# A chunked linear-attention recurrence and an expert mixture on one core: the triangular solves are placed one unit further ahead of their merge, x of four units is placed by products, TensorE gets filler products

## The chip, the core and the metric

The kernel runs on one NeuronCore of a Trainium2 chip. That core has TensorE (PE in the profile: matrix products into PSUM; PEld is its weight load), VectorE (DVE), ScalarE (ACT), GpSimd (POOL) and SyncE (SP), which here only issues DMAs. The metric is device time in microseconds: the median of the runs shown.

## The reference

All arrays are float32: batch B = 4, H = 8 heads, S = 768 tokens, head size D = 40. The first block is a recurrence over the tokens, for every batch and head:

```python
for t in range(S):
    y[:, :, t] = einsum('bhd,bhde->bhe', r_t, state)
    Sa = einsum('bhde,bhe->bhd', state, a_t)
    state = state * w_t[:, :, None, :] - einsum('bhd,bhe->bhde', Sa, b_t)
    state = state + einsum('bhd,bhe->bhde', v_t, k_t)
```

The second block takes x = y as a 3072 x 320 matrix (one row for each batch and token) and mixes four experts, with the probabilities of a row scaled to a sum of one:

```python
for e in range(4):
    h = maximum(x @ w1[e], 0)          # 320 x 1024
    out += p[:, e:e+1] * (h @ w2[e])   # 1024 x 320
```

## The kernel before

**Units.** The tokens are cut into 12 chunks of 64. A unit is one chunk of two batches, so that 2 x 64 tokens fill the 128 partitions; there are 24 units, two to a chunk (units 0 and 1 are chunk 0, and so on). `q.start` marks chunk 0, in which the state is still zero.

**The attention of a unit** is written as three generators, whose `yield`s are the places at which the code that calls them may stop.

- `within(q)` (L337) needs nothing of other units. It turns w (tile pw), scans it into running products G, turns G back (pg), scales a, b and k with it (gp and its reciprocal on VectorE, then tiles a_tok, n_tok, k_tok), turns these and r and v on TensorE (L368), and forms the 64 x 64 products F, E (pfe) and the scores (pc). F is the strictly triangular matrix whose inverse is needed. Its end forms EV (pev).
- `substitute(q, eng)` (L437) is the **solve**: the 32 x 32 blocks on the diagonal of F are gathered (blocks, L441), transposed in one instruction of VectorE (M, L445) and inverted by forward substitution, 16 steps of a product (L470) and a sum. On VectorE the sum is one reduction (L480), on GpSimd two additions (L483).
- `merge(q)` (L490) makes the 64 x 64 inverse QT of the two blocks: two transposes on VectorE (Qc, QTc), four copies on GpSimd (L503), then products pY and pQ on TensorE with a ScalarE copy behind each.
- `step(q)` (L530) is the part that hangs on the state, in five stages: prn and RH; psat (with SaT and SX behind it); pxr; pdy with Y and the new state; and stage five, which puts Y, that lies by head, into xT, that lies by the 320 columns. For unit 0 stage five is products with 0/1 matrices `pick` (pxT, L624) and one copy; for all others it is 10 to 12 DMAs on SP's queue (L636).

**The mixture** is cut into pieces that wait in the list `todo`, and `mix(n)` emits the next n. Units 0 and 1 go one by one (`mixture_of_unit`: `ups(e)` L651/L659 makes h, `down(e)` L698 the second product). From chunk 1 on, a whole chunk is mixed at once with a Strassen-like scheme (`mixture_of_chunk`, L763), which needs sums and differences of the blocks of w2 (`add_weights`, L735, five VectorE instructions for each expert) and of h (L757). Pieces of w1 come by DMA (`load_piece`, L237), w2 stays in SBUF (L254).

**What sets the order.** The loop from L879 on takes u = 1 to 23. In one turn it emits the first part of `within` of unit u+2, the rest of `within` of u+1, the last stages of `step` of u, all of `merge` and two stages of `step` of u+1, and the solve of u+2, with four gaps between them; `gap(n)` emits `add_weights` where `weights_at` says so, and then one or two pieces of the mixture (one where `sparse` says so). The first half of a solve is emitted at the end of a turn, the second at the start of the next one (the `yield` at L467), and its merge begins in that turn before gap 1. The solves of units 0, 3, 4 and 5 are on VectorE, the other twenty on GpSimd. The text of the program is a priority, not the order: each engine runs a queue that was fixed when the kernel was built, in which a later instruction may stand before an earlier one that is waiting. Instructions under `tc.keep_in_program_order` keep their order among themselves on their engine.

## Time and profile before

The median of three runs is 1178.29 us (1177.43 to 1181.34). The profiled execution took 1181.41 us, and its span on the core is 1179.7 us.

| | PE | PEld | DVE | ACT | POOL |
|---|---|---|---|---|---|
| busy us over the span | 1129.8 | 1005.5 | 698.1 | 364.5 | 462.4 |
| busy us, 5 to 50 us | 25.57 | 21.87 | 29.95 | 11.81 | 10.45 |
| busy us, 225 to 1030 us | 803.69 | 727.43 | 491.62 | 267.20 | 387.61 |

The mean granted clock of TensorE is 0.973; it is 0.70 from 5 to 50 us and 1.00 from 225 to 1030 us.

How to read it: in the table of stretches each line has the stretch and its length in us, then for each engine the busy us and, in brackets, the number of instructions, then the granted clock of TensorE (1.00 is full speed), the busy share of the 16 DMA engines, and GB/s. In the timeline a row has the start and the length in us, engine, line, operation, written tile <- read tiles, shapes and number of merged instructions, and in square brackets how long the engine had been idle before and what released it. A float32 product on TensorE shows as two MATMUL records, a transpose as one.

### The profile page before, as it was taken

The page shows a single profiled execution, that of the slowest core. Times are in us where ns is not written, and L with a number is a line of the kernel's source. Part 1 is how long each engine was busy: PE and PEld are TensorE (multiplying, and loading weights), DVE is VectorE, ACT ScalarE, POOL GpSimd, SP SyncE. Part 2 cuts the span into 40 slices and gives each one's busy share as a digit, 9 for nine tenths or more (in the row PEclk, how much of TensorE's full clock was granted, in tenths as well). Part 3 has the DMA queues.
Part 4 walks back from the last instruction along what each step waited for, and adds up shares of the span by engine and source line. Part 5 has one row for each costly group of instructions (what it writes and reads, how often), then busy time and mean ns, then how long its engine had stood idle before and what let it go on. Part 6 is the DMA issues. An engine that isn't in the chain of part 4 may idle for free.

```text
span 1179.7 us, 38554 instructions
## 1 busy us (share of the span) xinstructions
PE 1129.8 (96%) x16272; PEld 1005.5 (85%) x16272; DVE 698.1 (59%) x1503; ACT 364.5 (31%) x910; POOL 462.4 (39%) x1200
## 2 busy tenths in 40 slices
PE   4789996999999999999999999999999999999998
PEld 3668785899989989898998989999888998988887
DVE  6633787856646655755656566566466557543333
ACT  2323342333332333333333333333323333221110
POOL 4165000044734734625536436447347356250000
PEclk8689997999999999999999999999999999999999
DMA  4782633333333333342342332333333331221330
GB/s 67 200 239 68 141 64 86 78 108 68 95 94 84 96 95 81 92 103 73 95 95 63 108 89 73 107 78 89 90 93 90 93 91 58 76 86 51 103 89 12
DMA packets 220246, 108.03 MB, mean 92 GB/s; under 512 B 164090, under 2 KB 193450, under 8 KB 220074
## 3 DMA queue, kind: packets, MB, share of 16 engines
q1 hardware_dynamic: 220074, 105.56, 34.9%
q8 instruction: 129, 2.11, 0.7%
q14 instruction: 43, 0.35, 0.1%
HBM read 97.04 MB, written 3.93 MB: 86 GB/s over the span
## 4 chain that ended last, share of the span: by engine, by line
PE 86%; DVE 5%; POOL 3%; SPq 2%; issue 2%; DMA 1%; ACT 1%; POOLq 0%; DVEq 0%; ACTq 0%
PE p L763 27%; PE ph L659 27%; PE ph L651 8%; PE pdy L326 3%; PE po L698 2%; PE pfe L326 2%; PE prn L326 2%; POOL Z L483 2%; PE psat L326 2%; PE pxr L326 2%; SPq L188 1%; PE pQ L522 1%; PE pY L510 1%; POOL Z L470 1%; PE pc L326 1%
## 5 line engine op out<-in xcount | busy, mean ns | idle before, releaser
L659 PE MATMUL ph<-xT,w1p 128*128 128x256 f32 (+1 forms) x1520 | 342.8, 378 | 0.2 <-issue 0.2
L659 PEld LDWEIGHTS ph<-xT,w1p 128*128 128x128 f32 x1520 | 274.1, 190 | 62.8 <-issue 25.5
L757 DVE TENSOR_TENSOR a<-hs 128x512 f32<-128x512 f32 x220 | 149.9, 698 | 196.4 <-ACT hs L664 196.3
L483 POOL TENSOR_TENSOR Z<-Z 128x54 f32<-128x54 f32 (+14 forms) x640 | 217.4, 340 | 50.2
L664 ACT ACTIVATE hs<-ph 128x512 f32<-128x512 f32 (+1 forms) x208 | 117.4, 564 | 324.6 <-PE ph L659 323.5
L470 POOL TENSOR_TENSOR Z<-M,Z 128x62 f32<-128x62 f32 (+7 forms) x320 | 154.2, 482 | 89.5 <-DVE M L461 66.0
L677 DVE SCALAR_TENSOR_TENSOR osb<-p,gate,osb 128x320 f32<-128x320 f32 (+1 forms) x242 | 108.4, 486 | 110.4 <-PE p L763 103.2
L763 PE MATMUL p<-sums,a 128*128 128x160 f32 x1056 | 164.8, 299 | 0.0
L763 PEld LDWEIGHTS p<-sums,a 128*128 128x128 f32 x1056 | 152.9, 190 | 2.2
L441 POOL COPY blocks<-F 32x256 f32<-32x256 f32 x80 | 32.3, 404 | 276.6 <-ACT F L416 274.1
L651 PE MATMUL ph<-xT,w1p 64*128 64x256 f32 (+1 forms) x760 | 109.2, 399 | 4.9 <-issue 4.9
L503 POOL COPY QT<-QTc 32x256 f32<-32x256 f32 x96 | 37.7, 393 | 170.6 <-DVE QTc L497 160.7
L763 PE MATMUL p<-w,hs 128*128 128x160 f32 x704 | 102.8, 299 | 0.0
L763 PE MATMUL p<-w,a 128*128 128x160 f32 x704 | 102.8, 299 | 0.0
L763 PEld LDWEIGHTS p<-w,hs 128*128 128x128 f32 x704 | 100.3, 190 | 2.2
L763 PEld LDWEIGHTS p<-w,a 128*128 128x128 f32 x704 | 98.0, 190 | 0.0
L651 PEld LDWEIGHTS ph<-xT,w1p 64*128 64x128 f32 x760 | 67.3, 188 | 17.7 <-issue 7.8
L445 DVE STREAM_TRANSPOSE M<-blocks 128x1024 f32<-128x1024 f32 x24 | 47.1, 1964 | 26.0 <-POOL blocks L441 25.9
L364 DVE RECIPROCAL gp<-gp 128x320 f32<-128x320 f32 x24 | 51.5, 2145 | 0.0
L416 ACT COPY F<-pfe 128x256 f32<-128x256 f32 x48 | 15.5, 375 | 107.8 <-PE pfe L326 107.8
L592 ACT COPY RS<-pxr 64x256 f32<-64x256 f32 x88 | 32.2, 366 | 44.3 <-issue 25.3
L698 PE MATMUL po<-w,hs 128*128 128x320 f32 x128 | 44.0, 500 | 0.0
(140 smaller groups left out, 1406.8 us busy)
## 6 DMA issues: line engine op xcount, KB each, us to landing
w1p<-in_moe_w_dram SPq DMA_DIRECT2D x95, 512.0 KB
w1p<-in_moe_w_dram SPq DMA_DIRECT2D x190, 64.0 KB
w<-in_moe_w_dram SPq DMA_DIRECT2D x4, 1280.0 KB
sums<-in_moe_w_dram SPq DMA_DIRECT2D x9, 512.0 KB
natW<-in_w_dram SPq DMA_DIRECT2D x48, 80.0 KB
natA<-in_a_dram SPq DMA_DIRECT2D x48, 80.0 KB
natB<-in_b_dram SPq DMA_DIRECT2D x48, 80.0 KB
natK<-in_k_dram SPq DMA_DIRECT2D x48, 80.0 KB
```

What stands on the lines that cost most here:

```text
L326: nc.tensor.matmul(out=p[row][half(col), lo + at * out_cols:lo + (at + 1) * out_cols], lhsT=lhsT, rhs=rhs, start=(n == 0), stop=(n == len( ...
L364: nc.vector.reciprocal(out=gp[:], in_=gp[:])
L445: ins = nc.vector.transpose(out=M[:], in_=cols)
L470: ins = eng.tensor_tensor(out=Z[:, 1:3, 0:n, j + 1:Q], in0=M[:, j:j + 2, None, j + 1:Q].to_broadcast([P, 2, n, m]), in1=Z[:, here, 0:n, j: ...
L483: eng.tensor_tensor(out=z[:, 0], in0=z[:, 0], in1=z[:, x], op=ALU.add)
L651: nc.tensor.matmul(out=ph[i][:, f, :], lhsT=w1.last[i * DT:(i + 1) * DT, f, :], rhs=xT[i * DT:(i + 1) * DT, 2, :], start=(f == 0), stop=False,
L659: nc.tensor.matmul(out=ph[i][:, f, :], lhsT=w1.main[:, g, at * P:(at + 1) * P], rhs=xT[:, g, :], start=False, stop=(g == 1 and f == HF // ...
L664: nc.scalar.activation(out=h[:, i * HF // 2:(i + 1) * HF // 2, 0:n], in_=ph[i][:], func=ACTF.Relu,)
L677: nc.vector.scalar_tensor_tensor(out=to, in0=p, scalar=sc, in1=to, op0=ALU.mult, op1=ALU.add)
L698: nc.tensor.matmul(out=po[:], lhsT=hs[e][f // HF][:, f % HF, 0:P], rhs=w2_sb[e][:, f, :], start=(f == 0), stop=(f == NF - 1),)
L757: nc.vector.tensor_tensor(out=t[:], in0=x, in1=y, op=op)
L763: nc.tensor.matmul(out=p[:, n * HD:(n + 1) * HD], lhsT=a[:, f, :], rhs=b[:, f, :], start=(f == 0), stop=(f == HF - 1),)
```

## The change

- **Solve and merge.** `substitute` is no longer cut in two. In a turn of the loop the solve of u+2 now comes after gap 2, behind the first part (Qc, QTc, QT) of the merge of u+1, which has moved from before gap 1 to behind gap 2; the rest of the merge and two stages of `step` of u+1 follow it.
- **Engines.** Units 0 and 1 are solved on VectorE, units 2 to 23 on GpSimd. The four copies into blocks are now two on VectorE and two on ScalarE for every unit.
- **x.** Stage five of `step` places x by products for units 0 to 3 (`placed`), by DMAs for the rest.
- **Step.** Stage four (pdy, state) is emitted after gap 0 ahead of the next part of `within`. For chunk 0 the products pst of stage two get PSUM banks of their own.
- **Chunk 0.** Unit 1 takes the form of `within` that had been used from unit 2 on, with one more stop.
- **Weights.** `add_weights` stops after each instruction; the 20 instructions are dealt over gaps 1 of u = 2 to 2 of u = 5.
- **Filler.** `keep_warm(n)` emits n products of the identity with itself into a PSUM tile that nobody reads: 6 at the start, 4 behind the first part of unit 0's `within`, 36 behind the second part of unit 1's, all pinned.
- **Start.** The probabilities are loaded behind unit 1's a, b, k, v and r. The order of the calls ahead of the loop is written anew.

```diff
@@ -200,12 +200,13 @@
     minus_gate = const.tile([P, NC, B // 2, E], FP32, name="minus_gate")
     total = const.tile([P, NC, B // 2], FP32, name="total")
 
-    for bp in range(B // 2):
-        for i in range(2):
-            nc.sync.dma_start(
-                out=probs[bp * NC:(bp + 1) * NC, i],
-                in_=moe_domain_probs[(2 * bp + i) * S:(2 * bp + i + 1) * S, :].rearrange("(c t) e -> c t e", t=L),
-            )
+    def load_probs():
+        for bp in range(B // 2):
+            for i in range(2):
+                nc.sync.dma_start(
+                    out=probs[bp * NC:(bp + 1) * NC, i],
+                    in_=moe_domain_probs[(2 * bp + i) * S:(2 * bp + i + 1) * S, :].rearrange("(c t) e -> c t e", t=L),
+                )
 
     class Piece:
         pass
@@ -354,7 +355,7 @@
         nc.vector.tensor_tensor(out=q.gl[:], in0=q.gl[:], in1=G[:, :, L - 1:L], op=ALU.mult)
         yield
 
-        pg = by(turn("pg", tok(G))[:], 64)[:, :, 0:D]
+        pg = by(turn("pg", tok(G), q.u == 2)[:], 64)[:, :, 0:D]
         gp = sb.tile([P, H, D], FP32, name="gp")
         ins = nc.vector.tensor_tensor(out=gp[:], in0=pg, in1=n["W"][:, :, 0:D], op=ALU.mult)
         if q.u == 1:
@@ -381,7 +382,9 @@
                 if q.start:
                     tc.keep_in_program_order(ins)
 
-        if not q.start:
+        if q.u == 1:
+            yield
+        if q.u > 0:
             VT = turn_rv()
             yield
 
@@ -391,7 +394,7 @@
         )
         nc.vector.tensor_tensor(out=q.K[:, :, 0:D], in0=n["K"][:], in1=gp[:], op=ALU.mult)
         q.VC = VCs()
-        if not q.start:
+        if q.u > 0:
             nc.scalar.copy(out=q.VC[:, :, 0:D], in_=n["V"][:, :, 0:D])
         yield
 
@@ -400,7 +403,7 @@
         KT = turned("KT", q.K)
         yield
 
-        if not q.start:
+        if q.u > 0:
             causal_scores(VT)
             yield
 
@@ -419,7 +422,7 @@
             causal(of_slot(ET[:], s), pe[s])
         yield
 
-        if q.start:
+        if q.u == 0:
             tc.keep_in_program_order(nc.scalar.copy(out=q.VC[:, :, 0:D], in_=n["V"][:, :, 0:D]))
         q.EV = EVs()
         pev = quadrants(banks("pev"), 0, BY_TOKENS, D, lambda j, s, i: (
@@ -430,7 +433,7 @@
                 nc.scalar.copy(out=of_slot(q.EV[half(p)], i ^ p)[:, :, 0:D], in_=pev[i][half(p)])
         yield
 
-        if q.start:
+        if q.u == 0:
             causal_scores(turn_rv())
         yield
 
@@ -438,8 +441,8 @@
 
         blocks = sb.tile([P, H, Q], FP32, name="blocks")
         for i in range(P // Q):
-            ins = eng.tensor_copy(out=blocks[quarter(i)], in_=q.F[quarter(i), :, quarter(i % 2)])
-            tc.keep_in_program_order(ins)
+            move = nc.scalar.copy if i >= 2 else nc.vector.tensor_copy
+            tc.keep_in_program_order(move(out=blocks[quarter(i)], in_=q.F[quarter(i), :, quarter(i % 2)]))
         M = sb.tile([P, Q, Q], FP32, name="M")
         cols = blocks[:].rearrange("p h c -> p c h")[:, :, None, :].to_broadcast([P, Q, 4, H])
         ins = nc.vector.transpose(out=M[:], in_=cols)
@@ -463,8 +466,6 @@
         for x in (0, 3) if at_once else (0,):
             tc.keep_in_program_order(eng.tensor_copy(out=Z[:, x], in_=unit_cols[:]))
         for j in range(0, Q, 2):
-            if j == Q // 2:
-                yield
             n, m = j // 4 + 1, Q - 1 - j
             here = 3 * (j // 2 % 2) if at_once else 0
             ins = eng.tensor_tensor(
@@ -472,7 +473,7 @@
                 in1=Z[:, here, 0:n, j:j + 2].rearrange("p k x -> p x k")[:, :, :, None].to_broadcast([P, 2, n, m]),
                 op=ALU.mult,
             )
-            if j in (0, Q // 2):
+            if j == 0:
                 tc.keep_in_program_order(ins)
             z = Z[:, :, 0:n, j + 1:Q]
             if at_once:
@@ -485,7 +486,6 @@
 
             odd, even = (Z[:, x].rearrange("p k (r four) -> p k r four", four=4)[:, :, :, 1:3] for x in (3, 0))
             eng.tensor_copy(out=even, in_=odd)
-        yield
 
     def merge(q):
 
@@ -530,6 +530,8 @@
     def step(q, xT):
 
         st = [state[bb] for bb in q.b]
+
+        placed = q.c < 2
         if q.start:
             RH = q.EV
         else:
@@ -558,7 +560,8 @@
         ))
         SX = SXs()
         if not q.end:
-            pst = quadrants(p, NJ * L, BY_TOKENS, D, lambda j, s, i: (
+            at = (banks("pst"), 0) if q.start else (p, NJ * L)
+            pst = quadrants(*at, BY_TOKENS, D, lambda j, s, i: (
                 i ^ s, i, j, q.QT[half(i ^ s), head(j, s), :], RH[half(i ^ s), head(j, s), 0:D],
             ))
         SaT = sb.tile([P, NJ, 2, L], FP32, name="SaT", tag="step", bufs=3)
@@ -618,7 +621,7 @@
                 nc.vector.tensor_tensor(out=x, in0=x, in1=gl[:, :, i, :].to_broadcast([P, NJ, D]), op=ALU.mult)
         yield
 
-        if q.u == 0:
+        if placed:
             px = big("pxT")
             for n, (g, j) in enumerate(PLACES):
                 nc.tensor.matmul(
@@ -626,7 +629,7 @@
                     start=(n == 0 or PLACES[n - 1][0] != g), stop=(n + 1 == len(PLACES) or PLACES[n + 1][0] != g),
                 )
             nc.scalar.copy(out=xT, in_=px[:, 0:3 * P].rearrange("p (g t) -> p g t", g=3))
-        for h in range(H if q.u else 0):
+        for h in range(0 if placed else H):
             lo = h * D
             while lo < (h + 1) * D:
                 g, o = divmod(lo, P)
@@ -733,6 +736,7 @@
             (b[1, 0], b[1, 0], b[0, 0], ALU.subtract),
         ):
             tc.keep_in_program_order(nc.vector.tensor_tensor(out=to, in0=x, in1=y, op=op))
+            yield
 
     def mixture_of_chunk(qs, xT):
 
@@ -826,12 +830,24 @@
         q.xT = chunks_x[q.c][:, :, q.bp * P:(q.bp + 1) * P]
         return step(q, q.xT)
 
+    warm = big("warm")
+
+    def keep_warm(n):
+
+        for _ in range(n):
+            ins = nc.tensor.matmul(out=warm[:, 0:P], lhsT=ident[:], rhs=ident[:], start=True, stop=True)
+            tc.keep_in_program_order(ins)
+
     ws = [within(units[u]) for u in range(3)]
-    run(ws[0], 2)
+    keep_warm(6)
+    run(ws[0], 1)
+    keep_warm(4)
+    run(ws[0], 1)
     load(units[1], "ABKVR")
+    load_probs()
     run(ws[1], 1)
     run(ws[0], 2)
-    run(substitute(units[0], nc.vector))
+    substitute(units[0], nc.vector)
     run(ws[0], 1)
     set_pick()
     m, s = merge(units[0]), begin_step(0)
@@ -843,6 +859,8 @@
         load_piece()
         load_w2(e)
     run(ws[1], 1)
+    keep_warm(36)
+    run(ws[1], 2)
     load(units[2], "ABK")
     load_piece()
     for e in range(2, E):
@@ -851,31 +869,32 @@
     run(s, 4)
     run(ws[1], 1)
     run(s)
-    run(ws[1], 1)
-    run(substitute(units[1], nc.gpsimd))
+    run(ws[1], 2)
     mixture_of_unit(units[0])
+    substitute(units[1], nc.vector)
     normalize()
     run(ws[2], 1)
     run(ws[1])
+    mix(3)
+    m, s = merge(units[1]), begin_step(1)
+    run(m, 1)
     mix(1)
     run(ws[2], 2)
+    run(m)
     mix(1)
     run(ws[2], 2)
-    mix(1)
-    m, s = merge(units[1]), begin_step(1)
-    run(m, 1)
+    run(s, 2)
     run(ws[2], 1)
     load(begin(3), srcs)
-    run(substitute(units[2], nc.gpsimd))
-    run(m)
+    substitute(units[2], nc.gpsimd)
     mix(1)
-    run(s, 2)
-    mix(1)
-    w_next, solve = ws[2], iter(())
-
-    sparse = [4 * u + n for u in range(1, 4) for n in range(4)] + [16]
-
-    weights_at = {4 * 2 + 2: 0, 4 * 3 + 0: 1, 4 * 3 + 2: 2, 4 * 3 + 3: 3}
+    w_next = ws[2]
+
+    sparse = range(4 * 1, 4 * 4 + 2)
+
+    sums_at = {4 * 2 + n: 1 for n in range(1, 11)}
+    sums_at.update({4 * 4 + 3: 2, 4 * 5 + 0: 3, 4 * 5 + 1: 2, 4 * 5 + 2: 3})
+    sum_ops = (None for e in range(E) for _ in add_weights(e))
     for u in range(1, NU):
         q = units[u]
         m = s_next = w = iter(())
@@ -884,18 +903,17 @@
         if u + 2 < NU:
             w = within(units[u + 2])
 
-        def gap(n):
+        def gap(n, pieces=None):
             at = 4 * u + n
-            if at in weights_at:
-                add_weights(weights_at[at])
-            mix(1 if at in sparse else 2)
+            run(sum_ops, sums_at.get(at, 0))
+            mix((1 if at in sparse else 2) if pieces is None else pieces)
 
         run(w, 1)
         run(w_next)
         run(s, 1)
-        run(solve)
         gap(0)
 
+        run(s, 1)
         run(w, 1)
         run(s)
         if u == 1:
@@ -903,24 +921,23 @@
         elif q.bp:
             mixture_of_chunk(units[u - 1:u + 1], chunks_x[q.c])
         run(w, 1)
-        run(m, 1)
         gap(1)
 
         if u + 3 < NU:
             load(begin(u + 3), srcs)
         run(w, 2)
+        gap(2)
+
+        run(m, 1)
+        run(w, 1)
+        if u + 2 < NU:
+            substitute(units[u + 2], nc.gpsimd)
         run(m, 1)
         run(s_next, 1)
         run(m)
-        gap(2)
-
-        run(w, 1)
+        gap(3, 1)
         run(s_next, 1)
-        if u + 2 < NU:
-
-            solve = substitute(units[u + 2], nc.vector if u < 4 else nc.gpsimd)
-            run(solve, 1)
-        gap(3)
+        mix(0 if 4 * u + 3 in sparse else 1)
         s, w_next = s_next, w
     mix(len(todo))
     for piece in last:

```

## The prediction

> **What bounds the kernel now.** I read the slices of the page first (busy tenths of TensorE and its granted clock, 29.5 us each).
>
> ```profile
> PE   4789996999999999999999999999999999999998
> ...
> PEclk8689997999999999999999999999999999999999
> ```
>
> From the eighth slice on TensorE is busy and at full clock to the end; idle and slow-clock time both lie in the first seven, and the seventh has a hole. The table of stretches puts numbers on it:
>
> ```profile
> 50.00:74.00 24.00, 23.63 (x348) 20.03 (x341) 12.88 (x24) 9.58 (x24) 16.19 (x44) 1.00 0.94 277
> 74.00:90.00 16.00, 12.07 (x156) 7.71 (x148) 5.64 (x9) 2.10 (x6) 9.45 (x32) 0.68 0.82 210
> ...
> 114.00:122.00 8.00, 6.80 (x48) 4.53 (x46) 0.56 (x2) 1.37 (x4) 0.00 (x0) 0.79 0.30 101
> 122.00:179.00 57.00, 54.18 (x1024) 45.87 (x1024) 50.49 (x136) 23.39 (x67) 1.58 (x4) 1.00 0.47 95
> 179.00:198.00 19.00, 14.28 (x270) 11.11 (x272) 12.69 (x25) 4.14 (x11) 1.57 (x4) 0.73 0.26 47
> 198.00:211.00 13.00, 8.48 (x88) 6.45 (x78) 8.32 (x22) 3.07 (x10) 0.00 (x0) 0.74 0.55 146
> 211.00:225.00 14.00, 12.39 (x205) 10.46 (x204) 13.27 (x32) 5.92 (x16) 0.00 (x0) 0.88 0.37 109
> ...
> 225.00:1030.00 805.00, 803.69 (x12046) 727.43 (x12042) 491.62 (x1015) 267.20 (x665) 387.61 (x985) 1.00 0.34 88
> ```
>
> From 225 to 1030 us TensorE is busy 803.69 of 805 us at clock 1.00, while VectorE is at 61% and GpSimd at 48%: moving work among those gains nothing there. A gain can only lie before 225 us. The timeline names what ended the long idle times:
>
> ```profile
> 34.70 1.07 PE L510 MATMUL pY<-QTc,F 32*32 32x32 f32 x32 [11.86 <-DVE QTc L497]
> ...
> 78.17 1.06 PE L510 MATMUL pY<-QTc,F 32*32 32x32 f32 x32 [3.93 <-DVE QTc L497]
> ...
> 184.56 1.11 PE L294 MATMUL pNT<-ident,n_tok 128*128 128x128 f32 x4 [4.72 <-DVE n_tok L389]
> ...
> 203.37 3.02 PE L651 MATMUL ph<-xT,w1p 64*128 64x256 f32 x8 [4.52 <-issue]
> ```
>
> The first two are the solves of units 0 and 1, the third VectorE's queue, the fourth (no releaser named) xT: SP issues its 12 DMAs from 189.2 to 199.4 us, and ups begins behind them.
>
> **What slow clock costs.** After each hole the granted clock is about a half:
>
> ```profile
> 78.00:88.50 10.50, 10.33 (x78) 0.51 0.81 194
> 115.50:119.20 3.70, 3.56 (x16) 0.54 0.15 38
> 184.00:194.30 10.30, 9.74 (x174) 0.50 0.26 48
> 200.90:208.00 7.10, 4.63 (x12) 0.52 0.82 225
> 221.40:225.00 3.60, 3.60 (x60) 0.53 0.33 59
> ```
>
> The second product of a piece (po, L698) takes 6.10 us for 12 instructions from 83.12 us, 0.508 each, and 4.57 us for 16 from 131.32 us, 0.286 each: a ratio of 1.78. So a busy microsecond at half clock holds 1/1.78 of full-speed work, and 44% of it is lost: 4.5, 1.6, 4.3, 2.0 and 1.6 us in these five, 14.0 in all. The idle time of the stretches above (length less PE busy) is 0.4, 3.9, 1.2, 2.8, 4.7, 4.5 and 1.6 us. Together some 33 us are lost between 50 and 225 us.
>
> Here a rule is worth weighing. The idle time of 1.20 us before pQ at 115.64 us and that of 1.41 us before pdy at 220.22 us are each followed by a stretch at clock 0.54 or 0.53. The Trainium skill, "TensorE: Matmul & The Clock Gate", section "Why this matters for your kernels", asks only that idle gaps stay under about 3 us; by it these two would cost their 2.6 us alone, by the rows they cost 5.8. The rows decide: what is left of small waits counts double. The same page (Part 1) advises not to model the warm-up, as under 1% of a kernel; by that the filler could be left out. From 5 to 50 us the clock here is 0.70.
>
> **The change, part by part.**
>
> *Start, 5 to 50 us.* After pg of unit 1, TensorE idles 11.86 us (22.84 to 34.70) until unit 0's solve ends, then works at half clock until about 47 us. The 36 fillers are 72 passes; pxT (L624, 12 passes in 1.50 us at full clock, the last 0.275 long) gives 0.111 us a pass, so 8.0 us at full and 14.2 at half clock. If the clock rises after some 3.6 us (the shortest slow stretch above), 18 passes run at half clock and 54 at full, 9.6 us in all, and the fill ends at 32.4, ahead of 34.7. Then the chain from QTc to the first ups (34.56 to 51.66 us) runs at full clock. Its TensorE pieces take 1.07 (pY), 1.44 (pQ), 2.2 (psat), 1.45 (pxr), 3.25 (pdy) and 2.3 (AT, NT, KT), 11.7 us; the same pieces at full clock, from 110 to 150 us, take 0.69, 0.69, 1.1, 0.67, 1.8 and 1.47, 6.4 us. Bounds: 14.2 us of filler would make pY 2.4 us late (a loss of 2.4); all 5.3 and up to 1 us more, from SaT not waiting for pst and blocks on two engines, is 6.3. I take **-4.5**. The first ten fillers lie in waits for natW and G (to 4.76, 5.84 to 7.83): at nothing; if they overrun, under 1 us. The later load of the probabilities costs nothing: normalize reads them after 50 us.
>
> *Solve of unit 1.* On GpSimd its chain runs from 57.6 to 77.0 us, 19.4 us; unit 0's on VectorE took 10.7 us (22.8 to 33.5). pfe of unit 1 ends near 50.5 us, some 5 earlier with the start: F at 46, M and Z's preparation done at 51 (5 us, as from 17.7 to 22.7), the chain ends between 62 and, with other VectorE work between its links, 72. TensorE has pieces until about 72: ups, down, ups, down (some 20 us) and unit 1's and 2's attention. The hole of 3.9 and its half clock of 4.5 go. Next late is the ScalarE copy between pY and pQ, 0.9 us. **-7.5** (bounds 0, if the chain ends at 77 again, and -8.5).
>
> *Units 3, 4, 5 off VectorE, sums of w2 spread.* VectorE is busy 50.49 of 57 us from 122 to 179 and reaches n_tok of unit 4 only at 184.02, behind a solve, five L735 instructions (3.84 us) and a reciprocal (2.15). Without three solves (some 13 us each) that queue is gone. A GpSimd solve takes 19.8 us (85.4 to 105.3, unit 2), with blocks and M 24; the merge is now asked for a whole unit later, and a unit here takes about 33 us (pfe at 122.1 and at 155.8 us). So 4.7 of idle and 4.3 of clock go: **-8** (0 to -9). The copies QT on GpSimd are pinned ahead of the next solve, so they don't queue behind it. In the steady part the same cover is 45 us (a chunk takes 90.9): nothing. The blocks copies on ScalarE (two of about 0.36) stand between F and the copy of pY; prn (1.2 us of TensorE) covers that.
>
> *x of units 1 to 3.* 12 passes each: 1.50 us, **+4.5** on TensorE, which has no slack. They remove 36 SP issues of 0.7 us, and with them the hole at 198.85: 4.5 idle, 2.0 of clock, **-6.5** (bounds 0 and -6.5). Pieces of w1 behind them on SP come earlier.
>
> *Small waits*: 114 to 122 (2.8), 122 to 179 (2.8) and 211 to 225 (3.2): 8.8 us. They come from an order fixed at build against real durations, and the new order will have its own: half, **-4.4** (bounds +3 and -8.8).
>
> *Step four ahead, pst, stops in add_weights*: nothing where TensorE is full; the gap of one piece (4.4 to 5 us) that stays between psat and pxr, and between pxr and pdy, hides ScalarE's and VectorE's 1 to 2.4 us. In the sparse turns no piece follows psat; then pw and pev (1.1 us) stand against SaT (0.65): still nothing.
>
> **Sum**: -4.5 - 7.5 - 8 + 4.5 - 6.5 - 4.4 = -26.4 on the profiled execution of 1181.4: 1155.0. That execution lies 3.1 us above the median of 1178.3, so as a median **1152**.
>
> **Rivals.**
>
> *Half is given back at the start.* From 50 to 74 us the DMA engines are busy 0.94 at 277 GB/s: weights come in as fast as they can. With TensorE 4.5 us earlier, ups and down may wait for w1 and w2 by as much. And VectorE, 12.88 us busy there, gets 11.4 more of 24: unit 1's solve may end where it did, with nothing of the 7.5. Together 12 back: 1164. Against it: the loads are issued 8 to 20 us ahead of use, and no TensorE wait there names one.
>
> *The recurrence is what sets the pace*, and TensorE's holes only move: within 0.3%, 1178. Against it: TensorE is full from 225 us, so nothing else can be the pace there.
>
> *Slower: a wait in every unit.* Merge and step of u+1 now stand close together behind gap 2: pY, prn, pQ, then one piece, psat. If pY waits for QTc (VectorE behind the sums of gap 2: five L757 of 0.69 us) or pQ for its copy, TensorE loses time in each of 20 steady turns. 1.2 us idle with 1.6 of clock, as at 114.4, is 56 us: 1208. It decides from 26.4/20 = 1.3 us a unit. For it: the queue is fixed at build. Against it: in the steady part before, pY and prn stand in the same order and TensorE loses 1.3 us in 805; Qc and QTc are free to go in any of VectorE's waits (159 us for L757 alone).
>
> *The filler overruns*: 5 to 7 us of the start lost instead of gained: 1162; in the second case's range.
>
> **How the numbers follow.** The forecast's own range is 1143 to 1160, 0.58; the start given back or filler overrunning (1160 to 1174), 0.24; no change, 0.05; slower, 0.08; better than 1143 (all bounds at their best: -5.3 - 1 - 8.5 - 9 - 6.5 - 8.8 + 4.5 = -34.6, 1144), 0.05. The range 1143 to 1172 leaves out just under 0.2. A measurement of this kernel can tell some 0.3% (3.5 us) from no change: faster 0.87, same 0.05, slower 0.08.
>
> **What would show it.** Right: pY of unit 0 with less than 3 us of idle before it and clock 1.00 from about 35 us; first ups near 46; no wait of pY of unit 1, of n_tok, or of ph on xT above 1 us; 36 passes of pxT more; slices 2 to 7 at 9; and the stretch after the first chunk pieces as full as now. Wrong: a half clock after 50 us; PE idle in the steady part; TensorE waiting for w1p or w; QTc waiting for GpSimd in each turn with TensorE behind it.

## The result, and the profile after

The changed kernel takes 1211.28 us (median of 4 runs, 1206.07 to 1213.14) against 1179.61 (also 4 runs) for the kernel before it on the same chip: a ratio of 1.026 (95% interval 1.022 to 1.030). It is slower by 32 us, where the prediction said faster by 26. The profiled execution took 1213.14 us, with a span of 1211.4 us.

First the slices of the page of the kernel after (busy tenths of TensorE, granted clock, about 30 us each):

```profile
PE   7989999999999999999999999999999999999998
...
PEclk7989999899999999999999999999999999999999
```

By this view the change did what it was made for: slices 1, 2 and 7, which had a 4, a 7 and a 6, now have a 7 and two 9s (slice 3 keeps its 8). The loss isn't visible here, because 9 stands for 90% or more. The table of stretches shows it (kernel after; length, busy us of PE, PEld, DVE, ACT, POOL, clock, DMA share, GB/s):

```profile
50.00:74.00 24.00, 23.96 (x211) 19.53 (x211) 20.43 (x56) 6.41 (x18) 1.97 (x5) 1.00 0.98 290
74.00:90.00 16.00, 12.44 (x214) 11.33 (x214) 1.53 (x5) 5.99 (x17) 0.00 (x0) 0.79 0.93 264
114.00:122.00 8.00, 7.58 (x215) 6.55 (x216) 5.40 (x12) 3.89 (x12) 2.61 (x8) 1.00 0.32 53
122.00:179.00 57.00, 55.16 (x948) 45.92 (x947) 29.91 (x62) 23.37 (x66) 36.52 (x98) 1.00 0.40 94
179.00:198.00 19.00, 18.29 (x445) 15.05 (x443) 12.12 (x23) 10.07 (x27) 7.17 (x21) 1.00 0.46 112
198.00:211.00 13.00, 12.88 (x145) 10.86 (x137) 8.64 (x19) 5.45 (x13) 11.04 (x26) 1.00 0.22 63
211.00:225.00 14.00, 13.09 (x194) 11.08 (x196) 10.53 (x24) 3.81 (x8) 5.02 (x14) 1.00 0.39 87
225.00:1030.00 805.00, 784.06 (x11389) 692.85 (x11390) 470.08 (x988) 269.35 (x669) 348.50 (x898) 0.99 0.32 83
```

The last line stands against 803.69 of 805 us and 12046 matmuls before: 657 matmuls fewer in the same time. That is where the gain was lost.

**Before 225 us.** From 114 to 225 us TensorE is idle for 4.0 us at full clock; before it was idle for 14.9 and lost 9.5 more to slow clock. From 50 to 90 us the wait for unit 1's solve is gone, but a new one stands in its place, for w1p at 75.42 us (3.55 us), and half clock behind it. The first `ups` starts at 48.1 us instead of 51.7. Adding up: 3.6 at the start, 2.3 between 50 and 90 (8.8 lost before, 4.3 idle and 4.5 by clock; now 3.6 idle and 2.9 by clock, 44% of 6.6 busy us at half clock), 20.4 less 4.5 for the added x products between 114 and 225: a lead of some 21.8 us. From there to the end 53 us are lost.

**The steady part.** The same steady unit now takes 47.41 us, before 45.45 (from pY to the next unit's pY). Two excerpts of the timeline show the difference: first the kernel before, then the one after.

```profile
595.99 1.29 POOL L503 COPY QT<-QTc 32x256 f32<-32x256 f32 x3
...
597.62 0.69 PE L326 MATMUL pc<-RT,VT 64*64 64x64 f32 x32
598.25 0.69 PE L510 MATMUL pY<-QTc,F 32*32 32x32 f32 x32
598.87 0.68 PE L326 MATMUL prn<-state,AT 64*64 64x40 f32 x32
```

```profile
610.65 0.69 PE L327 MATMUL pfe<-NT,AT 64*64 64x64 f32 x32
...
611.22 0.68 DVE L761 TENSOR_TENSOR a<-hs 128x512 f32<-128x512 f32 x1
611.74 0.70 PE L654 MATMUL ph<-xT,w1p 64*128 64x256 f32 x2
611.82 0.38 DVE L680 SCALAR_TENSOR_TENSOR osb<-p,minus_gate,osb 128x160 f32<-128x160 f32 x1
...
612.12 0.61 DVE L495 STREAM_TRANSPOSE Qc<-Z 128x256 f32<-128x256 f32 x1
...
612.76 0.45 DVE L497 STREAM_TRANSPOSE QTc<-Qc 128x256 f32<-128x256 f32 x1
...
613.26 0.69 PE L510 MATMUL pY<-QTc,F 32*32 32x32 f32 x32 [0.82 <-DVE QTc L497]
613.34 1.85 POOL L503 COPY QT<-QTc 32x256 f32<-32x256 f32 x4 [20.14 <-DVE QTc L497]
```

Before, QTc had long been there when pY's turn came. After, Qc and QTc stand on VectorE right behind the sums a (L761) and the osb (L680) of gap 2, and pY waits 0.82 us for QTc. That isn't because the solve is late: GpSimd had been idle for 20.14 us when QTc came (last line). Nor is VectorE full; it is at 58% there. Qc could have run for some 19 us (GpSimd's last work ended at 593.2), and VectorE's fixed queue held it back; e1 below tests this. The waits by pair, kernel after:

```profile
PE pY L510 <- DVE QTc L497: 15.3, 19, 0.8
PE pQ L522 <- issue: 4.2, 3, 1.7
PE ph L654 <- DMA w1p<-in_moe_w_dram: 3.5, 1, 3.5
...
PE ph L654 <- issue: 2.0, 1, 2.0
...
PE prn L327 <- issue: 1.5, 1, 1.5
```

The first line is 15.3 us in 19 units. Counted from start to start on TensorE the wait costs about 1.05 us a unit. The other 0.9 of the 1.96 is regrouping, that is, another sequence of small products (32 or 64 rows) and large ones. pfe and psat, once one run, are now apart, and two of the eight products of a group ph stand between pfe and pY. From the last product of a small group to the first of a large one, or back, it is 0.12 to 0.31 us; from pfe to psat it was 0.04. All such steps together, without the wait, take 5.4 us in the unit after and 4.8 in the unit before; 0.3 more is lost inside the divided ph.

**Holes without a releaser.** The three lines with "issue" are something else. Rows of the timeline and of the table of stretches, kernel after:

```profile
711.47 0.45 PE L327 MATMUL prn<-ident,state 64*64 64x64 f32 x11 [1.55 <-issue]
```

```profile
712.90:716.30 3.40, 3.40 (x11) 2.25 (x8) 0.52 (x2) 1.04 (x4) 2.34 (x9) 0.50 0.08 13
```

There are five such holes: 1.71 us ending at 227.94, 1.15 at 327.73, 1.55 at 711.47, 1.32 at 810.00 and 2.01 at 909.66, each followed by half clock for 3.4 to 6.8 us. The units that hold them are 3.2 to 5.2 us longer than 47.41, some 20 us in all. Four lie inside the run pfe, pY, prn, pQ (192 small products with as many weight loads, two ph among them), the fifth two ph products behind it. The sum for the steady part: 17 units from the sixth pY to the 23rd lose 1.96 each, 33 us, and the five holes 20; measured are 51.7 (774.8 us before, 826.5 after; two units of before are 0.8 and 1.0 us long themselves).

What the holes are: the page lists a DMA queue that carries no data of the kernel but instructions (kernel after; packets, MB, share of the 16 engines' span):

```profile
q8 instruction: 130, 2.13, 0.7%
```

130 transfers of 16 KB during the span. In the five places one of them begins 2.5 to 2.7 us before the hole ends: 225.39, 325.25, 708.84, 807.50 and 906.96 us. That spread is narrow, while the holes themselves are 1.15 to 2.01 us long; it fits a TensorE that has used up its instructions and waits for a fetch of fixed length. The places fit too. Counted in TensorE's records (products and weight loads), the holes come after about 6753, 9533, 20410, 23189 and 25970 of them, which is 11, 43, 11 and 11 times 253 apart; and 32800 records over 130 transfers are 252 a transfer. So the holes stand where one transfer's worth of instructions ends. Experiment e4 tests this. The Trainium skill, "Runtime: NRT & Kernel Launch", section "Instruction fetch mechanics", has the instructions fetched during the run in blocks of 16 KiB, and calls the cost of passing from one block to the next mostly hidden; this trace agrees on the blocks, and in these five places the cost is 1.15 to 2.01 us of idle time.

### The profile page after: what moved, and what is told of

It reads as the page before. It is cut to its first block, busy times and chain, and to the rows that moved or that the text cites. A ratio compares the mean times of both kernels' runs of the same rounds, so it can differ in the third digit from the quotient of the medians.

```text
span 1211.4 us, 38747 instructions
## 1 busy us (share of the span) xinstructions
PE 1167.4 (96%) x16400; PEld 1026.1 (85%) x16400; DVE 684.9 (57%) x1465; ACT 387.7 (32%) x961; POOL 465.0 (38%) x1218
## 4 chain that ended last, share of the span: by engine, by line
PE 89%; DVE 5%; SPq 2%; ACT 2%; issue 1%; DMA 1%; ACTq 0%; DVEq 0%
PE ph L662 29%; PE p L767 28%; PE ph L654 8%; PE pdy L327 3%; PE po L701 2%; PE psat L327 2%; PE prn L327 2%; PE pxr L327 2%; DVE osb L680 1%; PE pc L327 1%; PE pQ L522 1%; PE pY L510 1%; SPq L188 1%; PE pg L295 1%; PE pev L327 1%
## 5 line engine op out<-in xcount | busy, mean ns | idle before, releaser
L662 PE MATMUL ph<-xT,w1p 128*128 128x256 f32 (+1 forms) x1520 | 352.7, 386 | 0.1
L662 PEld LDWEIGHTS ph<-xT,w1p 128*128 128x128 f32 x1520 | 280.7, 195 | 66.1 <-issue 25.8
L484 POOL TENSOR_TENSOR Z<-Z 128x31 f32<-128x31 f32 (+7 forms) x704 | 245.2, 348 | 55.2
L761 DVE TENSOR_TENSOR a<-hs 128x512 f32<-128x512 f32 x220 | 149.6, 697 | 169.9 <-ACT hs L667 169.9
L680 DVE SCALAR_TENSOR_TENSOR osb<-p,gate,osb 128x320 f32<-128x320 f32 (+1 forms) x242 | 108.4, 486 | 214.8 <-PE p L767 207.9
L471 POOL TENSOR_TENSOR Z<-M,Z 128x62 f32<-128x62 f32 (+7 forms) x352 | 158.7, 451 | 118.6 <-DVE M L464 92.7
L654 PE MATMUL ph<-xT,w1p 64*128 64x256 f32 (+1 forms) x760 | 123.0, 404 | 5.9 <-DMA w1p<-in_moe_w_dram 3.5
L654 PEld LDWEIGHTS ph<-xT,w1p 64*128 64x128 f32 x760 | 72.2, 189 | 21.4 <-issue 11.2
L419 ACT COPY F<-pfe 128x256 f32<-128x256 f32 x48 | 15.5, 375 | 92.0 <-PE pfe L327 92.0
L398 ACT COPY VC<-natV 128x320 f32<-128x320 f32 x23 | 10.6, 460 | 104.9 <-PE pdy L327 98.2
L327 PE MATMUL pdy<-VC,k_tok 64*64 64x104 f32 (+1 forms) x768 | 39.0, 261 | 0.0
```

The lines of the kernel that those rows point to most:

```text
L327: nc.tensor.matmul(out=p[row][half(col), lo + at * out_cols:lo + (at + 1) * out_cols], lhsT=lhsT, rhs=rhs, start=(n == 0), stop=(n == len( ...
L471: ins = eng.tensor_tensor(out=Z[:, 1:3, 0:n, j + 1:Q], in0=M[:, j:j + 2, None, j + 1:Q].to_broadcast([P, 2, n, m]), in1=Z[:, here, 0:n, j: ...
L484: eng.tensor_tensor(out=z[:, 0], in0=z[:, 0], in1=z[:, x], op=ALU.add)
L654: nc.tensor.matmul(out=ph[i][:, f, :], lhsT=w1.last[i * DT:(i + 1) * DT, f, :], rhs=xT[i * DT:(i + 1) * DT, 2, :], start=(f == 0), stop=False,
L662: nc.tensor.matmul(out=ph[i][:, f, :], lhsT=w1.main[:, g, at * P:(at + 1) * P], rhs=xT[:, g, :], start=False, stop=(g == 1 and f == HF // ...
L680: nc.vector.scalar_tensor_tensor(out=to, in0=p, scalar=sc, in1=to, op0=ALU.mult, op1=ALU.add)
```

## The experiments

The theory after this reading: the part ahead of 225 us gains about what was forecast, and the new order of a turn loses it again in every unit (QTc behind gap 2, regrouping, code fetches). The rivals: the loss is in other parts of the change (copies on ScalarE, the DMA-limited weights), or the code fetch is a fiction and the long holes are something of the data. All ratios are to the kernel before.

**e1: the transposes back ahead of gap 2.**

```diff
         run(w, 2)
+        run(m, 1)
         gap(2)

-        run(m, 1)
         run(w, 1)
```

> The changed kernel with one line moved: the first part of merge (Qc, QTc, QT) is emitted ahead of gap 2 instead of behind it. Theory (queue): in every turn pY waits because QTc stands on VectorE behind the five sums a and the four additions to osb of gap 2; then the wait of 0.82 us before pY is gone in all turns, the period of a unit falls from 47.4 to about 46.3 us, and the long waits right behind pY (1.2 to 2.0 us with half clock after them) get rarer, since the window of the clock no longer holds two holes: 1170 to 1192 us. Rival (regrouping): the time goes where TensorE changes more often between 64x64 and 128-row products; then the period stays above 47 us and the time at 1203 to 1211 us.

Measured: 1199.62 us, 1.017 (1.013 to 1.020), 12 us better than after and between the two ranges expected. The wait of pY is gone, so VectorE's queue was its cause, but a unit still takes 46.62 us. Timeline of e1:

```profile
610.84 0.69 PE L510 MATMUL pY<-QTc,F 32*32 32x32 f32 x32
...
610.96 0.65 ACT L419 COPY F<-pfe 128x256 f32<-128x256 f32 x2 [4.86 <-PE pfe L327]
...
611.64 0.81 ACT L445 COPY blocks<-F 32x256 f32<-32x256 f32 x2
...
612.48 0.75 ACT L516 COPY Yq<-pY 32x256 f32<-32x256 f32 x2
...
612.89 1.07 PE L522 MATMUL pQ<-Yq,Qc 32*32 32x32 f32 x32 [0.27 <-ACT Yq L516]
```

With QTc on time the next late thing shows: pQ waits for Yq, which stands on ScalarE behind F and the two copies into blocks that the change put there. pQ takes 1.07 instead of 0.69 us and starts 0.27 late: about 0.66 a unit. In the kernel after this cost nothing only because pY was late itself.

**e8: as e1, with all four copies into blocks on VectorE.**

```diff
-            move = nc.scalar.copy if i >= 2 else nc.vector.tensor_copy
+            move = nc.vector.tensor_copy
```

> The changed kernel with the first part of merge ahead of gap 2 and all four copies into blocks on VectorE instead of two on ScalarE. In the run with the transposes moved alone, pQ waits 0.66 us in each unit, for the copy of pY, which stands on ScalarE behind F and the two blocks copies (0.81 us). Theory (queue on ScalarE): that wait goes, period 46.0 instead of 46.6 us, 1184 to 1193 us. Rival (pQ is held by something else): 1196 to 1202 us.

Measured: 1191.03 us, 1.009 (1.007 to 1.012). A unit takes 45.90 us, 0.72 less: ScalarE's queue was the next wait. The remaining 0.45 over 45.45 has no wait with a name; 0.3 of it lies in the steps between groups on TensorE (5.1 us a unit, before 4.8). So the two queues, VectorE's and ScalarE's, account for 1.5 of the 1.96 us. The 8.6 us won are less than 20 times 0.72, since long holes at "issue" remain and are longer here: seven of 1.5 to 3.0 us between 315 and 940 us.

**e2: the turn of before, the new start.** The loop's body is that of the kernel before, with the solve whole ahead of gap 3; all else is of the kernel after.

```diff
         gap(0)
 
-        run(s, 1)
         run(w, 1)
...
         run(w, 1)
+        run(m, 1)
         gap(1)
...
         run(w, 2)
+        run(m, 1)
+        run(s_next, 1)
+        run(m)
         gap(2)

-        run(m, 1)
         run(w, 1)
-        if u + 2 < NU:
-            substitute(units[u + 2], nc.gpsimd)
-        run(m, 1)
-        run(s_next, 1)
-        run(m)
-        gap(3, 1)
         run(s_next, 1)
-        mix(0 if 4 * u + 3 in sparse else 1)
+        if u + 2 < NU:
+            substitute(units[u + 2], nc.gpsimd)
+        gap(3)
```

> The changed kernel with the turn of the loop as it was before (merge of u+1 from before gap 1 to before gap 2, step four behind the next part of within, the solve emitted whole ahead of gap 3), and with all of the new start: filler, two solves on VectorE, x of four units by products, sums of w2 spread. Theory (the loss is in the turn, the gain in the start): the 26 us gained by the eighteenth ups are kept, period 45.5 us: 1148 to 1158 us. Rival (the start only moves the holes, or the later solves on GpSimd cost the steady part): 1175 us or more.

Measured: 1199.89 us, 1.016 (1.014 to 1.019). The expectation of 1148 to 1158 failed, though its reason held in one half: from 345 us on a unit takes 45.45 us and nothing more is lost. The loss is in the first turns (the unit from 294.57 to 345.01 us still takes 50.4). Timeline of e2:

```profile
241.68 0.52 POOL L484 TENSOR_TENSOR Z<-Z 128x8 f32<-128x8 f32 x2
242.23 0.61 DVE L495 STREAM_TRANSPOSE Qc<-Z 128x256 f32<-128x256 f32 x1 [10.55 <-POOL Z L484]
...
243.67 1.06 PE L510 MATMUL pY<-QTc,F 32*32 32x32 f32 x32 [10.60 <-DVE QTc L497]
```

Here QTc is late because GpSimd's solve has only just ended. There are four more such waits of pY (5.07, 4.28, 2.48 and 0.94 us; 23.4 in all), most with half clock behind them. So the late merge isn't only a cost: while the turns are short and their solves are on GpSimd it is needed.

**e3: the start of before, the new turn.** The mirror image: the kernel before with the body of the loop of after alone; the solves of units 3 to 5 stay on VectorE, blocks on GpSimd.

> The kernel before with the turn of the loop as the change has it (merge behind gap 2, step four ahead), and nothing else of the change; solves of units 3 to 5 stay on VectorE. Theory: each of some 20 steady turns loses 2.0 us, and some turns lose 3 to 5 us more in a long wait: 1215 to 1240 us. Rival (filler, products for x or the solves make the steady part slow): 1176 to 1185 us.

Measured: 1221.85 us, 1.035 (1.031 to 1.038). A unit takes 47.54 us, with pY's 0.82 in each. The new turn alone costs 41 us, and the rest of the change gains 10 on top of it. It excludes the copies on ScalarE and the new start as the cause of the steady loss, for e3 has its copies on GpSimd and the start of before.

**e4: the code shifted.** 32 more filler products at the very start, so that every later instruction of TensorE lies 64 products and their weight loads further on.

```diff
-    keep_warm(6)
+    keep_warm(38)
```

> The changed kernel with 38 instead of 6 filler products at the very start: 64 products and 64 weight loads more on TensorE's queue, half of a 256-instruction block of code, and nothing else. Theory (code loading): the five long waits without a releaser (226, 326, 709, 808, 907 us; 1.2 to 2.0 us) come where the dense products pY, prn, pQ run over the end of a loaded block; with all code shifted by half a block they fall in other units, or elsewhere in the same turn; the 0.82 us before pY stay in every turn. Time 1195 to 1216 us. Rival (they come from data or a queue): they stay in the same units.

Measured: 1215.09 us, 1.028 (1.023 to 1.033), the same as after within what the runs scatter. Timeline of e4:

```profile
517.99 0.69 PE L510 MATMUL pY<-QTc,F 32*32 32x32 f32 x32 [0.82 <-DVE QTc L497]
521.47 0.77 PE L522 MATMUL pQ<-Yq,Qc 32*32 32x32 f32 x25 [1.46 <-issue]
```

The 0.82 us before pY stay in every unit. The long holes move to other units: they now end at 521.47 and 622.16 us (2.04), where the kernel after has none, with fetches that begin at 518.9 and 619.4, again 2.5 to 2.7 earlier; those near 711, 810 and 909 us are gone, and smaller ones stand at 278.9 and 865.5 (0.55 and 0.41). Counted as above, these four, in order of time, come after about 8271, 15102, 17880 and 24707 records: 6, 33, 44 and 71 times 253 behind the first hole of the kernel after. So these holes hang on where the instructions lie, at the ends of blocks of one size, and not on the data or on the order of the work. That the time is that of the fetch is supported by the timing; it wasn't taken away by itself. Half clock isn't tied to the long holes alone: in e4 the unit from 764.84 us is 3.6 us longer, at half clock from 767.4 to 774.2 us, with no idle time but the 0.83 before pY and 0.25 before pQ.

**e5: late merge for the short turns alone.** From e1, e2 and e3 follows a version: the turn of the kernel after up to u = 5, the turn of before (as in e2) from u = 6 on.

```diff
+        if u <= 5:
...
+        else:
...
```

> The changed kernel, but only turns 1 to 5 of the loop have the changed order; from turn 6 on the order of before stands (merge of u+1 from before gap 1, step four behind the next part of within, solve emitted ahead of gap 3). Theory: in the first turns a solve on GpSimd needs the late merge, in the steady ones the early merge costs nothing and the late one 2 us a unit and code-loading holes. By the starts of pY of units 2 to 5 the changed kernel is about 20 us ahead when the steady part begins, and that is kept: 1153 to 1166 us, period 45.5 us from the seventh unit on. Rival (the early merge waits for GpSimd's solve in the steady part too, or the start's lead is only work put off): 1175 us or more.

Measured: 1167.54 us, 0.989 (0.986 to 0.992): faster than both kernels, by 12 and by 44 us, and just above the range expected. From the ninth pY on (357.5 us) most units take 45.4 to 45.5 us.

The next kernels take the parts of the start out of this version one at a time.

**e6: as e5 without filler.** `keep_warm` emits nothing.

> As the kernel with the changed order in turns 1 to 5 only, and without any filler product. By the forecast's term the filler is worth 4.5 us at the start: 3 to 8 us above that kernel, with the first ups at 51 us instead of 46 to 48. Rival (what the filler gains is lost again at the wait for weights at 75 us): within 2 us of it.

Measured: 1163.95 us, 0.987 (0.984 to 0.989), in neither of the two ranges. The two intervals overlap: no gain by the filler can be seen in the time. The first `ups` starts at 49.1 us instead of 46.2, but the sixth at 77.2 instead of 78.2, for in e5 this row stands in between:

```profile
78.15 0.95 PE L654 MATMUL ph<-xT,w1p 64*128 64x128 f32 x8 [2.63 <-DMA w1p<-in_moe_w_dram]
```

Whoever arrives 3 us earlier waits for the weights 3 us longer; the DMA share is 0.99 from 50 to 74 us in both. Taking the filler out also moves the code by 184 records, and the long holes fall elsewhere (e5 has 1.45 us before 227.41, e6 2.70 before 85.80), so a few us either way can't be told apart here.

On the clock at the start the profile misleads. e12 below and e6 have the same instructions in the same order on TensorE far beyond this place; by the table of stretches e12 was at half clock here and e6 was not, first e12, then e6:

```profile
37.00:40.50 3.50, 2.95 (x96) 2.84 (x95) 1.45 (x3) 1.94 (x6) 0.00 (x0) 0.50 0.26 39
```

```profile
37.00:40.50 3.50, 2.95 (x97) 2.85 (x97) 1.41 (x3) 1.97 (x7) 0.00 (x0) 1.00 0.22 37
```

But busy time and count are the same, and so is the time of pY just ahead. The rows of e12, e6 and e5:

```profile
34.21 1.06 PE L510 MATMUL pY<-QTc,F 32*32 32x32 f32 x32 [3.19 <-DVE QTc L497]
```

```profile
34.17 1.06 PE L510 MATMUL pY<-QTc,F 32*32 32x32 f32 x32 [3.00 <-DVE QTc L497]
```

```profile
32.41 0.69 PE L510 MATMUL pY<-QTc,F 32*32 32x32 f32 x32 [0.24 <-ACT RT L369]
```

So TensorE ran at the slow rate in e12 and in e6, and the 1.00 of e6 is wrong there; only e5, with filler, had pY at full rate. From pY to the first `ups` it is 13.8 us in e5 and in the kernel after, 15.0 in e6, 15.5 in e12 and 17.0 in the kernel before. The filler is worth 1.2 to 1.7 us on this way, which then wait at w1p.

**e7: as e5, x of units 1 to 3 by DMA.**

```diff
-        placed = q.c < 2
+        placed = q.u == 0
```

> As the kernel with the changed order in turns 1 to 5 only, but x of units 1 to 3 is placed by DMAs as before. By the forecast the products cost 4.5 us on TensorE and save 6.5 (a hole of 4.5 and its half clock): 2 us above that kernel, with ups waiting for xT of unit 3 again. Rival (with VectorE free of the solves the DMAs are hidden): 3 to 5 us below it.

Measured: 1176.87 us (10 runs), 0.997 (0.996 to 0.999). The products are worth 9.3 us net, more than either expectation. Without them `ups` waits 4.07 us at 190.56 us behind SP's 12 issues (181.1 to 190.0 us), and pY of unit 2 waits 5.03 us at 115.11; why that solve is asked for too early here wasn't followed up.

**e9: as e6, units 3 to 5 on VectorE again** (`nc.vector if u < 4 else nc.gpsimd` in the early turns).

> As e6 (1163.95 us), but the solves of units 3, 4 and 5 are on VectorE again, as in the kernel before. The prediction gave 8 us to their leaving VectorE (with the sums of w2 spread, which stay spread here). If that term holds, VectorE is full again between 110 and 180 us, n_tok is late, and the time is 1168 to 1174. Rival: the late merge and the spread sums alone had freed VectorE's queue; then the time stays at 1162 to 1166.

Measured: 1177.64 us (10 runs), 0.998 (0.995 to 1.000): 13.7 us worse than e6, more than expected, and by another path than the n_tok that the expectation named. Timeline of e9:

```profile
135.18 1.56 ACT L595 COPY RS<-pxr 64x256 f32<-64x256 f32 x4 [3.31 <-DVE SX L334]
...
136.77 0.66 ACT L667 ACTIVATE hs<-ph 128x256 f32<-128x256 f32 x2
...
137.21 0.98 PE L654 MATMUL ph<-xT,sums 64*128 64x128 f32 x6 [2.84 <-ACT hs L667]
```

VectorE works on SX between the links of the solve (it ends near 135.9 us), ScalarE's RS waits for SX, hs stands behind RS on ScalarE, and TensorE waits for hs. The same again at 176.57 us (3.28). n_tok is late too, by 1.14 us at 225 us.

**e10: as e6, unit 1 on GpSimd.** `substitute(units[1], nc.gpsimd)`.

> As e6 (1163.95 us), but unit 1 is solved on GpSimd, as in the kernel before. The prediction gave 7.5 us to that solve on VectorE: 1169 to 1173 if the term holds, with pY of unit 1 waiting some 4 us for QTc near 78 us. Rival, half is given back at the start: weights arrive no sooner than 79 us, and the wait for them takes what the solve's wait took; then 1162 to 1167.

Measured: 1170.46 us, 0.993 (0.991 to 0.996): 6.5 us worse than e6, and in its timeline pY of unit 1 waits again:

```profile
76.29 1.07 PE L510 MATMUL pY<-QTc,F 32*32 32x32 f32 x32 [3.85 <-DVE QTc L497]
```

**e11 and e12: two finer cuts of e6.** e11 emits Qc and QTc ahead of gap 2 in turns 1 to 5 (the edit of e1, in the early turns); e12 goes over to the turn of before at u = 5 (`if u <= 4`).

> As e6 (1163.95 us), but in turns 1 to 5, which have the late merge, Qc and QTc are emitted ahead of gap 2, as e1 did in all turns. If pY waits there for VectorE's queue (about 1 us in each of 5 turns) and no more, 1159 to 1163. Rival: in these short turns the solve on GpSimd ends only about when gap 2 does, so that Qc, pinned ahead, waits for GpSimd and holds VectorE's and then TensorE's work: 1166 to 1180, with idle time before pY near 110 to 235 us.

> As e6 (1163.95 us), but the late merge ends with turn 4 instead of 5. e2, with the old turn everywhere, waited 10.6 us before pY at 233 us and still 0.9 us at 293.6 us. If the merge of the seventh unit needs the late place, the time is 1166 to 1176 with a hole before pY near 220 to 235 us; if the sparse turns (1 to 3) alone need it, 1161 to 1164.

Measured: 1161.74 us, 0.987 (0.983 to 0.990), and 1161.45 us, 0.986 (0.983 to 0.989). Neither can be told from e6. In e11 no wait of pY is left behind 35 us (e6 has 0.82 at 222.8 and 0.83 at 270.2), so its rival falls: the solves do end before gap 2. And the merge of the seventh unit doesn't need the late place when the turns before it are not disturbed. (In e2 that unit waited 0.94 us; the 10.6 that the expectation names stood before the sixth unit's pY.) The best versions are 1.3 to 1.4% faster than the kernel before.

## Why the prediction was wrong

**The step that failed** is one sentence of the part by part working: "In the steady part the same cover is 45 us (a chunk takes 90.9): nothing." It asked whether GpSimd's solve would be done in time. It was, by some 19 us. It didn't ask behind what the transposes would now stand on VectorE. The rival "a wait in every unit" named exactly that (QTc behind the sums of gap 2, for 20 units, 1208 us) and got 0.08. What it set against it was that Qc and QTc "are free to go in any of VectorE's waits". They aren't: the queue is fixed when the kernel is built, and the text had said so itself. Free time on an engine helps an instruction only if its place in the queue comes before that time. The prediction gave 1.2 us idle and 1.6 of clock a unit as the rival's price; measured are 0.82 idle (1.05 from start to start) without loss of clock, 0.9 from regrouping, and the long holes. That its 1208 lies near the 1211 measured is luck: almost the same sum from other terms.

**"prn (1.2 us of TensorE) covers that"** (blocks on ScalarE ahead of the copy of pY) was wrong too, and hidden by the first mistake. Once e1 takes QTc's wait away, it costs 0.66 us a unit; e8 takes 8.6 us off.

**"Step four ahead, pst, stops in add_weights: nothing where TensorE is full"** left out what the new order does to runs of small products. It had no price for changes of shape or for fetches of code. The trace of before has holes at "issue" too, of 0.35 us at 646.67 and 0.65 at 874.21. One more was in the prediction's hands: the 1.20 us before pQ at 115.64 us, from which it priced the rival, ends 2.8 us after a code transfer begins, 16 times 253 records ahead of the first hole of the kernel after. It took that for a wait that comes from the order.

**Before 225 us** the sum was nearly right: -26.4 forecast, some -21.8 measured. Its terms, one at a time:

| term | forecast | measured |
|---|---|---|
| start, filler | -4.5 | first ups 3.6 earlier, 1.2 to 1.7 of it by the filler (e5 against e6 and e12); given back at w1p |
| solve of unit 1 on VectorE | -7.5 | -6.5 without filler (e10 against e6); -2.3 in the kernel after, since w1p is late |
| units 3 to 5 off VectorE | -8 | -13.7 (e9 against e6) |
| x by products, net | -2.0 | -9.3 (e7 against e5) |
| 114 to 225 us, all terms there | -14.4 | -15.9 |

The terms taken out one by one (6.5, 13.7 and 9.3) add up to more than the 15.4 us by which e6 is ahead of the kernel before: they aren't independent. A late part moves the next wait into the open (e7's pY at 115 us, e2's five waits), so each alone undoes some of the others. "Half is given back at the start", the first rival, was right in its first half: weights come as fast as they can, and what reaches them sooner waits. Its second half fell; unit 1's solve does end in time.

**The working on the filler** had the fill itself nearly right (9.6 us forecast, 9.9 measured, and no wait of pY behind it above 0.3 us). But it had the whole way from QTc to the first `ups` at full clock, 5.3 us to gain there, of which it took 4.5; the clock falls again behind the fill (0.51 from 37.00 to 40.50 us in the kernel after). The way is 3.2 us shorter than before, and 1.2 to 1.7 of that is the filler's.

**What stays open.** The 0.9 us a unit for regrouping is read from start times; no run changes the grouping alone. The fetch of code was moved (e4) but not removed, and it moves in every run that adds or takes products (e6 and e7 against e5), so their differences hold some of it. Why one hole is followed by half clock and another isn't stays open. Whether the cuts of e11 and e12 are worth a microsecond can't be told from these runs.

## What to carry to other kernels

When an instruction moves in the program's text, ask two things: whether its inputs are ready, and behind which instructions it now stands on its own engine; an engine at 58% still makes others wait if the queue is fixed. Price a wait that repeats by its count before giving it a chance: 1.96 us in each of 17 units, 33 us, outweighed the 22 us gained before. And if a reordering helps a part of the run where one resource is short and harms the part where it isn't, use each order where it pays: e5, e11 and e12 have the steady unit of before again and keep 12 to 18 of the 22 us.

## What the runs showed of the hardware

- TensorE's instructions come by DMA during the run, 130 transfers of 16 KB in the kernel after. In the seven long holes looked at there and in e4, the hole ends 2.5 to 2.7 us after such a transfer begins (2.3 to 2.4 in the seven of e8), whole multiples of about 253 records lie between the holes, and shifting the code moves them. All seven lie in or just behind a run of small products with as many weight loads.
- In the kernel after, a hole of 1.15 to 2.0 us in a busy stretch is followed by half clock for 3.4 or 6.8 us (0.50 from 712.90 to 716.30 us). On the other hand holes of 2.04 and 1.76 us in e1 (before 470.98 and 945.44 us) left it at 1.00, and there the products behind them run at full rate. The Trainium skill, "TensorE: Matmul & The Clock Gate", Part 1, has the clock fall after at least one idle window of about 3.4 us. The length of the slow stretches agrees with a window of that size; that the clock falls after 1.55 us and stays up through 2.04 doesn't follow from the length of the idle time alone.
- The granted clock in the profile can be wrong at the start: it is 1.00 for e6 at 34 us, where the 32 products of pY take 1.06 us as in e12 at 0.50, against 0.69 in e5. The 0.70 given for 5 to 50 us of the kernel before holds such a part too: at 8.74 us four products pw take 1.06 us at a clock shown as 1.00, in the kernel after 0.60. Product times of the same shape settle it.
- From the last product of a group of small products to the first of a group of large ones, or back, it is 0.12 to 0.31 us; from pfe to psat, both 64x64, 0.04.
